# Score bursts in tiles of 64 rows by 64 columns, both row blocks of a part in turn

## The chip, the cores and the metric

One Trainium2 chip, one core. The metric is device time in microseconds. The profiler's span of an execution is about 1.9 us less than the time of the same execution (568.3 against 570.23 for the profiled run of before), so spans are compared with spans and times with times.

## The reference

Attention with a threshold, then a gated feed-forward layer, 8 batches x 8 heads x 576 rows, head size 64:

```python
scores = matmul(q, k.transpose(0, 1, 3, 2)) / sqrt(64)
scores = where(scores >= max(scores, -1) - tau, scores, -1e9)
attn   = exp(scores - max(scores, -1));  attn /= sum(attn, -1) + 1e-9
x      = matmul(attn, v)                  # to rows of 8 heads x 64 = 512
xn     = x / sqrt(mean(x * x) + 1e-6) * rms_g
out    = (silu(xn @ w_gate) * (xn @ w_val)) @ w_out     # 512 -> 1536 -> 512
```

Only `q @ k.T` is touched here. It is computed in fp32, since the threshold is sharp.

## The kernel before

The kernel lists its operations, orders them per engine in a scheduler of its own (`order_ops`) and then emits them in that order. One step is 128 rows of two heads: a "score burst" on TensorE fills two stretches of PSUM, `s_ps[0]` and `s_ps[1]`, one per head ("bank 0" and "bank 1" below); VectorE reads each (`ttr`: scale, minimum, copy to SBUF); GpSimd, ScalarE and VectorE make the weights from it. There are 144 steps: 128 of main rows, 16 of the last 64 rows of two batches.

```python
def emit_s(s):
    ...
    if kind == "m":      # 128 main rows: one row block
        outs = [(slice(0, 128), b % 2, lambda hs: qkT[b % 2][p][hs, 0, c])]
    else:                # last 64 rows of two batches: two row blocks, each with keys of its own
        outs = [... (HALF[e], e, lambda hs, e=e: qTv[b % 2][hs, p, HALF[e]]) ...]

    def fn(o):
        for rows, i, lhs in outs:
            for part in range(2):            # 576 keys in two parts of 288
                for h in range(2):           # the head: SBUF partitions 0-63 or 64-127
                    hs, n = HALF[h], S // 2
                    nc.tensor.matmul(s_ps[h][rows, ROW_AT + n * part:ROW_AT + n * part + n], lhs(hs),
                                     kT[i][p][h][hs, n * part:n * part + n], start=True, stop=True)

    for h in range(2):
        deps.append(ttr_of.get((s - 1, h)))   # VectorE must have read this bank of the step before
```

The contraction has 64 rows, so each head uses half the array's rows (a row tile) and the two heads run side by side. With 128 output rows the tile is 64 rows by 128 columns; with 64 it is 64 by 64, and two blocks of 64 output rows lie in two column tiles. (Where the texts speak of the "row tiles of a part in turn", they mean these row blocks.) Operations carry a `mode`: 1 for 64x128 tiles (main bursts and the fp32 transposes of q and k, L303, L438, L462 in the traces), 2 for bursts of the last rows, 0 and 3 for full-height products.

Of the kernel before, what the change touches and what calls it, by code (L numbers as in the profile page):

```python
# [24 lines left out]


class Op:
    __slots__ = ("eng", "cost", "prio", "deps", "fn", "ring", "frees", "slot", "end", "start", "dma", "opens", "nring", "mode", "bulk", "release", "pick")

    def __init__(self, eng, cost, prio, deps, fn, ring=None, frees=None, dma=0.0, nring=1, mode=0, bulk=False):  # L30
        self.eng, self.cost, self.prio, self.fn = eng, cost, prio, fn
        self.deps = [d for d in deps if d is not None]
        self.ring, self.frees, self.dma = ring, frees, dma
        self.slot = self.end = self.start = None
        self.opens = ()
        self.nring = nring
        self.mode = mode
        self.bulk = bulk
        self.release = 0.0
        self.pick = None  # L40


def order_ops(ops, ring_sizes):


    import heapq

    ring_free = {r: [(0.0, i) for i in range(n)] for r, n in ring_sizes.items()}
    users = {}
    left = {}  # L50
    for i, o in enumerate(ops):
        left[i] = len(o.deps)
        for d in o.deps:
            users.setdefault(id(d), []).append(i)
    pending = {}
    for i, o in enumerate(ops):
        pending.setdefault(o.eng, [])
        if not left[i]:
            pending[o.eng].append(i)
    eng_free = {e: 700.0 for e in pending}  # L60
    dma_free = 0.0
    mode = 0
    out = []
    ready_at = {i: 0.0 for i in range(len(ops))}
    while len(out) < len(ops):
        best = None
        for e, lst in pending.items():
            if not lst:
                continue
            t0 = eng_free[e]  # L70
            cand = None
            for i in lst:
                o = ops[i]
                t = max(t0, ready_at[i])
                if o.ring is not None:
                    free = [f for f in ring_free[o.ring] if o.pick is None or f[1] in o.pick]
                    if len(free) < o.nring:
                        continue
                    t = max(t, sorted(free)[o.nring - 1][0])
                other = e == "PE" and o.mode != mode  # L80
                t = max(t, o.release)
                if o.bulk:
                    t = max(t, dma_free - BACKLOG)
                k = (t + (BIAS if other else 0.0), o.prio, i)
                if cand is None or k < cand:
                    cand = k
            if cand is not None and (best is None or cand < best[0]):
                best = (cand, e)
        (t, _, i), e = best
        o = ops[i]  # L90
        cost = o.cost
        if e == "PE":
            if o.mode != mode:
                t -= BIAS
                cost += SWITCH
            mode = o.mode
        o.start = t
        if o.ring is not None:
            o.slot = []
            for _ in range(o.nring):  # L100
                got = min(f for f in ring_free[o.ring] if o.pick is None or f[1] in o.pick)
                ring_free[o.ring].remove(got)
                o.slot.append(got[1])
        eng_free[e] = t + cost
        if o.dma:
            dma_free = max(dma_free, t + 300.0) + o.dma
            o.end = max(dma_free, t + o.cost) + (LAT_TR if o.cost == COST["sp_tr"] else LAT_LD if o.bulk else 2000.0)
        else:
            o.end = t + cost
        if o.frees is not None:  # L110
            ring_free["R"].append((o.end + SEM, o.frees[0].slot[o.frees[1]]))
        for slot in o.opens:
            ring_free["R"].append((o.end + SEM, slot))
        pending[e].remove(i)
        out.append(o)
        for j in users.get(id(o), []):
            u = ops[j]
            wait = 0.0 if u.eng == o.eng and not o.dma else SEM + (SLACK if u.eng == "PE" else 0.0)
            ready_at[j] = max(ready_at[j], o.end + wait)
            left[j] -= 1  # L120
            if not left[j]:
                pending[u.eng].append(j)
    return out
# [3 lines left out]
def kernel(  # L127
# [26 lines left out]
    def sb(name, shape, dt=FP32):  # L154
        return konst.tile(shape, dt, tag=name, name=name)

    def ps(name, n):
        return psum.tile([128, n], FP32, tag=name, name=name)
# [14 lines left out]
    qkT = [[t[:, p].rearrange("p (j s) -> p j s", j=2)[:, :, 0:MAIN].rearrange("p j (c n) -> p j c n", n=128)  # L173
            for p in range(NP)] for t in qkt]
    kT = [[[t[:, p, S:2 * S], t[:, p, MAIN:MAIN + S]] for p in range(NP)] for t in qkt]
    kTt = [[t[:, :, S + MAIN:2 * S], t[:, :, MAIN:S]] for t in qkt]
    qTv = [sb(f"qTv{i}", [128, NP, 128]) for i in range(2)]
# [30 lines left out]
    ring = [ps(f"ring{i}", 512) for i in range(4)]  # L208
    ring += [s_ps[h][:, 512 * i:512 * (i + 1)] for h in range(2) for i in range(2)]
    HALF = (slice(0, 64), slice(64, 128))  # L210
# [9 lines left out]
    def add(eng, cost, prio, deps, fn, **kw):  # L220
        o = Op(eng, cost, prio, deps, fn, **kw)
        ops.append(o)
        return o
# [11 lines left out]
    for s, (ci, p) in enumerate(steps):  # L235
        kind, b, _ = chunks[ci]
# [309 lines left out]
    def emit_s(s):  # L546
        ci, p = steps[s]
        kind, b, c = chunks[ci]
        if kind == "m":
            deps = qk_ready[b, p, c] + kt_ready[b, p]  # L550

            outs = [(slice(0, 128), b % 2, lambda hs: qkT[b % 2][p][hs, 0, c])]
        else:
            deps = list(qv_ready[b])
            outs = []
            for e in range(2):
                deps += qk_ready[2 * b + e, p, 0] + kt_ready[2 * b + e, p]
                outs.append((HALF[e], e, lambda hs, e=e: qTv[b % 2][hs, p, HALF[e]]))

        def fn(o):  # L560
            for rows, i, lhs in outs:
                for part in range(2):
                    for h in range(2):

                        hs, n = HALF[h], S // 2
                        nc.tensor.matmul(s_ps[h][rows, ROW_AT + n * part:ROW_AT + n * part + n], lhs(hs),  # L566
                                         kT[i][p][h][hs, n * part:n * part + n], start=True, stop=True)

        for h in range(2):
            deps.append(ttr_of.get((s - 1, h)))  # L570
        o = add("PE", COST["s_main" if kind == "m" else "s_virt"], s, deps, fn, mode=1 if kind == "m" else 2)
        if REL_N[0] <= s < REL_N[1]:
            o.release = REL[0] + REL[1] * s
        if kind == "m":
            last_s[("k", b, p)] = [o]
        else:
            last_sv[b, p] = [o]
            for e in range(2):
                last_s.setdefault(("k", 2 * b + e, p), [])
                last_s["k", 2 * b + e, p] = last_s["k", 2 * b + e, p] + [o]  # L580
        return o
# [327 lines left out]
    for c in range(DFF // 512):  # L909
        for d in range(0, 4, 2):  # L910
            for w_dram, w_sb in ((moe_w_gate, wg), (moe_w_val, wv)):
                slot = n // 2 % len(stage)
# [20 lines left out]
    for j in range(4):  # L933
        o = add("POOL", COST["pool_dma"], W_FROM + W_STEP * n + j + WO_AT, [], lambda o, j=j: nc.gpsimd.dma_start(
            out=wo[:, 3 * j:3 * j + 3], in_=wo_src[:, 3 * j:3 * j + 3]), dma=DMA_NS['wo'], bulk=True)
# [3 lines left out]
    for s, (ci, p) in enumerate(steps):  # L939
        kind, b, c = chunks[ci]  # L940
        so = s_of[s] = emit_s(s)
        emit_softmax(s, so)
        if p % 2:
            emit_av(s)
        if p == NP - 1:
            gi, j = place[ci]
            xt_op[ci] = emit_x(ci, s, gi % NXT, 128 * j)
            if ci in last_of:
                g = groups[last_of[ci]]
                emit_ffn(last_of[ci] % NXT, [(ci_of[x], xt_op[ci_of[x]]) for x in g], s + (ELAG if place[ci][0] < NELAG else LAG), PACE,  # L950
                         last_of[ci] >= len(groups) - STREAMED)
            for bb in ([b] if kind == "m" else [2 * b, 2 * b + 1]):
                left[bb] -= 1
                if not left[bb] and bb + 2 < B:
                    emit_batch_inputs(bb + 2)
# [4 lines left out]
    for h in range(2):  # L960
        ttr_of[len(steps) - 1, h].opens = OPENS[h]
    seq = order_ops(ops, {"R": 4})
    global LAST_SEQ
    LAST_SEQ = seq
    with tc.manual_schedule():
# [77 lines left out]
```

## Time and profile before

| | before |
|---|---|
| time, median of 3 runs | 567.91 us (567.86 to 568.21) |
| span of the profiled execution | 568.3 us |
| TensorE busy, share of the chain that ended last | 98%, 89% |
| score bursts (L566) in that chain | 28% |
| VectorE waiting for score bursts | 60.5 us |

The chain is the work that ended last, followed back from the last instruction to whatever released each step. A record is one pass of a matmul in the trace, and a start stamp is its recorded start. A row of groups reads: line, engine, operation, out<-in, tile (rows*columns), shape, count, then busy us and mean ns, then idle time before it and what ended it. The prediction shows the rows themselves.

### The profile page before, as it was taken

What the parts mean: (1) busy time and instruction counts of PE and PEld (TensorE: products, weight loads), DVE (VectorE), ACT (ScalarE), POOL (GpSimd) and SP (SyncE); (2) the same over time, 40 slices, a digit from 0 to 9 for tenths busy, and PEclk for the clock granted to TensorE, in tenths of its full rate; (3) what the DMA queues carried; (4) which work ended last, traced back from release to release, by engine and by line L of the source; (5) the groups of instructions that cost most, each with busy time, mean ns of one, the idle gap of its engine ahead of it and who ended that gap; (6) DMA issues with size and microseconds to landing.
All of it is one profiled execution on the core that took longest, in us unless ns stands there. A gap on an engine that the chain in (4) does not pass through costs nothing.

```text
span 568.3 us, 13686 instructions
## 1 busy us (share of the span) xinstructions
PE 558.4 (98%) x5000; PEld 334.7 (59%) x5000; DVE 427.2 (75%) x1093; ACT 457.4 (80%) x739; POOL 322.4 (57%) x462
## 2 busy tenths in 40 slices
PE   8999999999999999999999999999999999999997
PEld 4666766767676555555555555545555455454674
DVE  4899977969958588758895789659875886586354
ACT  4999899999878787979898898778978897884332
POOL 2378946976747457666766658555666555551000
PEclk9999999999999999999999999999999999999999
DMA  8999998769994686999876799789887565633211
GB/s 187 250 289 282 178 195 184 161 132 202 167 202 104 136 159 149 177 177 187 178 160 148 142 186 181 161 168 162 174 167 184 88 96 86 178 81 44 84 37 38
DMA packets 270019, 88.98 MB, mean 157 GB/s; under 512 B 252544, under 2 KB 262272, under 8 KB 269952
## 3 DMA queue, kind: packets, MB, share of 16 engines
q1 hardware_dynamic: 267168, 86.02, 74.1%
q0 software_dynamic: 1600, 1.57, 1.8%
q8 instruction: 39, 0.64, 0.5%
q10 hardware_dynamic: 1184, 0.52, 0.3%
q14 instruction: 28, 0.23, 0.1%
HBM read 37.75 MB, written 9.44 MB: 83 GB/s over the span
## 4 chain that ended last, share of the span: by engine, by line
PE 89%; DVE 3%; DMA 2%; issue 2%; ACT 2%; POOL 1%; SPq 0%; DVEq 0%; POOLq 0%; ACTq 0%
PE s_ps L566 28%; PE ring L792 16%; PE ring L797 16%; PE ring L853 14%; PE ring L697 6%; PE ring L303 2%; PE ring L693 2%; DVE ssb L589 2%; DMA qkn<-in_q_dram 1%; PE s_ps L831 1%; PE s_ps L853 1%; PE ring L659 1%; PE s_ps L797 1%; PE ring L364 1%; DMA stage<-in_q_dram 1%
## 5 line engine op out<-in xcount | busy, mean ns | idle before, releaser
L589 DVE CUSTOM_DVE_ANT_0 ssb<-s_ps,zrow 128x576 f32<-128x576 f32 x288 | 207.8, 754 | 67.7 <-PE s_ps L566 60.5
L607 ACT ACTIVATE ssb<-ssb,nth 128x576 f32<-128x576 f32 x224 | 165.9, 766 | 32.4 <-POOL nth L596 32.1
L566 PE MATMUL s_ps<-qkt 64*128 64x288 f32 x1024 | 170.2, 429 | 1.4 <-DVE mx L589 1.1
L566 PEld LDWEIGHTS s_ps<-qkt 64*128 64x128 f32 x1024 | 96.2, 186 | 53.5 <-DVE mx L589 16.2
L640 POOL TENSOR_SCALAR wsb<-ssb,nth 128x576 f16<-128x576 f32 x64 | 110.5, 1726 | 9.7 <-DMA wt<-wsb 2.9
L792 PE MATMUL ring<-xnT,wg 128*128 128x512 f16 (+1 forms) x548 | 112.9, 328 | 0.4 <-DVE sl L809 0.4
L797 PE MATMUL ring<-xnT,wv 128*128 128x256 f16 (+1 forms) x544 | 111.4, 327 | 0.6 <-ACT qTv L472 0.3
L596 POOL TENSOR_SCALAR nth<-mx 128x2 f32<-128x2 f32 x144 | 31.6, 220 | 133.9 <-DVE mx L589 120.6
L809 DVE SCALAR_TENSOR_TENSOR sl<-th,ring 128x512 f32<-128x512 f32 (+1 forms) x137 | 75.9, 554 | 25.9 <-ACT th L806 24.6
L614 ACT ACTIVATE wsb<-ssb 128x1152 f16<-128x1152 f32 x80 | 92.9, 1161 | 1.9
L806 ACT ACTIVATE th<-ring 128x512 f32<-128x512 f32 (+1 forms) x137 | 66.3, 486 | 28.9 <-PE ring L792 26.4
L853 PE MATMUL ring<-wo,hf 128*128 128x512 f16 x384 | 89.3, 380 | 0.0
L645 POOL TENSOR_TENSOR wsb<-wsb,esb 128x576 f16<-128x576 f16 x64 | 81.8, 1278 | 8.8 <-ACT esb L626 4.4
L814 DVE TENSOR_TENSOR hf<-ring,sl 128x256 f16<-128x256 f32 (+1 forms) x136 | 75.9, 558 | 10.0 <-PE s_ps L566 0.5
L797 PEld LDWEIGHTS <-wv 128*128 128x128 f16 x576 | 52.2, 98 | 42.9 <-issue 12.3
L792 PEld LDWEIGHTS <-wg 128*128 128x128 f16 x576 | 52.0, 98 | 41.0 <-issue 11.6
L853 PEld LDWEIGHTS <-hf 128*128 128x128 f16 x408 | 37.4, 98 | 47.2 <-issue 6.6
L626 ACT ACTIVATE esb<-ssb,nth 128x576 f16<-128x576 f32 x64 | 49.2, 768 | 7.1 <-POOL nth L596 7.0
L697 PE MATMUL ring<-va,wt 128*128 128x65 f16 (+1 forms) x1264 | 52.8, 193 | 0.0
L697 PEld LDWEIGHTS <-wt 128*128 128x128 f16 (+1 forms) x1280 | 48.7, 100 | 3.4
L611 ACT ACTIVATE wsb<-ssb 128x576 f16<-128x576 f32 x64 | 43.6, 681 | 1.6
L693 PE MATMUL ring<-va,wt 128*128 128x130 f16 (+1 forms) x158 | 35.1, 227 | 0.1
(68 smaller groups left out, 448.1 us busy)
## 6 DMA issues: line engine op xcount, KB each, us to landing
vst<-in_v_dram SPq DMA_DIRECT2D x32, 256.0 KB, 3.2
qkn<-in_k_dram SPq DMA_DIRECT2D x31, 256.0 KB, 3.8
out_dram<-osb SPq DMA_DIRECT2D x31, 256.0 KB, 2.6
qkn<-in_q_dram SPq DMA_DIRECT2D x28, 256.0 KB, 4.1
stage<-in_moe_w_gate_dram SPq DMA_DIRECT2D x6, 512.0 KB, 6.6
stage<-in_moe_w_val_dram SPq DMA_DIRECT2D x6, 512.0 KB, 6.3
wt<-wsb SPq DMA_TRANSPOSE x128, 3.1
wo<-in_moe_w_out_dram POOLq DMA_DIRECT2D x4, 384.0 KB, 7.6
```

The lines of the kernel that those rows point to most:

```text
L566: nc.tensor.matmul(s_ps[h][rows, ROW_AT + n * part:ROW_AT + n * part + n], lhs(hs), kT[i][p][h][hs, n * part:n * part + n], start=True, st ...
L589: nc.vector.tensor_tensor_reduce(out=ssb[a][:, h], in0=s_ps[h][:, ROW_AT:ROW_AT + S], in1=zrow, scale=-1.0 / 8.0, scalar=3.0e38, op0=ALU.a ...
L607: nc.scalar.activation(out=ssb[a][:, h], in_=ssb[a][:, h], func=PRELU, scale=-1.0, bias=nth[m][:, h:h + 1], **PRELU_KW)
L614: nc.scalar.activation(out=wsb[s % NW], in_=ssb[a], func=AF.Exp)
L640: nc.gpsimd.tensor_scalar(out=wsb[s % NW][:, h], in0=ssb[a][:, h], scalar1=nth[m][:, h:h + 1], scalar2=None, op0=ALU.is_le)
L645: nc.gpsimd.tensor_tensor(out=wsb[s % NW][:, h], in0=wsb[s % NW][:, h], in1=esb[es], op=ALU.mult)
L697: nc.tensor.matmul(ring[o.slot[0]][rs, at:at + D + 1], w[:, 5 * h + j, rs], va[vi][:, p, 2 * j + h], start=False, stop=(h == 1 and j == 3))
L792: nc.tensor.matmul(ring[o.slot[0]][:, 0:n], wg[d][:, fs], xnT[slot][:, d, 0:n], start=(d == 0), stop=(d == 3))
L797: nc.tensor.matmul(ring[o.slot[0]][:, 0:n], wv[d][:, fs], xnT[slot][:, d, 0:n], start=(d == 0), stop=(d == 3))
L809: nc.vector.scalar_tensor_tensor(out=sl[i][:, 0:n], in0=th[i][:, 0:n], scalar=1.0, in1=ring[g.slot[0]][:, 0:n], op0=ALU.add, op1=ALU.mult)
L814: nc.vector.tensor_tensor(out=hf[hi][:, 0:n], in0=ring[vv.slot[0]][:, 0:n], in1=sl[i][:, 0:n], op=ALU.mult)
L853: nc.tensor.matmul(ring[(first or o).slot[0]], hf[hs[fc][0]][:, 128 * j:128 * (j + 1)], wo[:, fc], start=(fc == 0), stop=(fc == NFC - 1))
```

## The change

The intent: a burst with no 64x128 transposes behind it leaves the tiling in any case, so it may as well use the tiles of the last rows' bursts, whose first weight load is half as wide. Both row blocks of a part now come in turn.

```diff
         if kind == "m":
-            outs = [(slice(0, 128), b % 2, lambda hs: qkT[b % 2][p][hs, 0, c])]
+            whole = [(slice(0, 128), b % 2, lambda hs: qkT[b % 2][p][hs, 0, c])]
+            quads = [(rs, b % 2, lambda hs, rs=rs: qkT[b % 2][p][hs, 0, c, rs]) for rs in HALF]
 ...
         def fn(o):
-            for rows, i, lhs in outs:
-                for part in range(2):
+            for part in range(2):
+                for rows, i, lhs in quads if kind == "v" or o.quad else whole:
                     for h in range(2):
 ...
     seq = order_ops(ops, {"R": 4})
+    on_pe = [o for o in seq if o.eng == "PE"]
+    for o, after in zip(on_pe, on_pe[1:]):
+        o.quad = after.mode != 1
```

More of the change, by code (lines that the diff above doesn't have):

```diff
@@ L27 @@
 class Op:
-    __slots__ = ("eng", "cost", "prio", "deps", "fn", "ring", "frees", "slot", "end", "start", "dma", "opens", "nring", "mode", "bulk", "release", "pick")
+    __slots__ = ("eng", "cost", "prio", "deps", "fn", "ring", "frees", "slot", "end", "start", "dma", "opens", "nring", "mode", "bulk", "release", "pick", "quad")
     def __init__(self, eng, cost, prio, deps, fn, ring=None, frees=None, dma=0.0, nring=1, mode=0, bulk=False):
@@ L40, in __init__ @@
         self.pick = None
+        self.quad = False
 def order_ops(ops, ring_sizes):
@@ L550, in emit_s @@
             deps = qk_ready[b, p, c] + kt_ready[b, p]
-            outs = [(slice(0, 128), b % 2, lambda hs: qkT[b % 2][p][hs, 0, c])]
+            whole = [(slice(0, 128), b % 2, lambda hs: qkT[b % 2][p][hs, 0, c])]
+            quads = [(rs, b % 2, lambda hs, rs=rs: qkT[b % 2][p][hs, 0, c, rs]) for rs in HALF]
         else:
             deps = list(qv_ready[b])
-            outs = []
+            quads = []
             for e in range(2):
                 deps += qk_ready[2 * b + e, p, 0] + kt_ready[2 * b + e, p]
-                outs.append((HALF[e], e, lambda hs, e=e: qTv[b % 2][hs, p, HALF[e]]))
+                quads.append((HALF[e], e, lambda hs, e=e: qTv[b % 2][hs, p, HALF[e]]))
         def fn(o):
-            for rows, i, lhs in outs:
-                for part in range(2):
+            for part in range(2):
+                for rows, i, lhs in quads if kind == "v" or o.quad else whole:
                     for h in range(2):
```

## The prediction

> **What bounds the kernel now.** I read the page first, its head, its busy shares and its chain that ended last, because a change to one engine's instructions is worth something only where that engine sets the end.
>
> ```profile
> span 568.3 us, 13686 instructions
> PE 558.4 (98%) x5000; PEld 334.7 (59%) x5000; DVE 427.2 (75%) x1093; ACT 457.4 (80%) x739; POOL 322.4 (57%) x462
> PE 89%; DVE 3%; DMA 2%; issue 2%; ACT 2%; POOL 1%; SPq 0%; DVEq 0%; POOLq 0%; ACTq 0%
> ```
>
> TensorE (PE) is busy 98% of the span and carries 89% of the chain; the next engine, ScalarE, is busy 80%. The granted clock is full in all 40 slices. The ends of matmuls are modelled, so 98% alone would prove little, and I work with starts only. Next, the table of groups with shapes kept apart, to see what the score bursts (L566) cost and what waits there.
>
> ```profile
> L566 PE MATMUL s_ps<-qkt 64*128 64x288 f32 x1024 | 170.2, 429 | 1.4 <-DVE mx L589 1.1
> L566 PE MATMUL s_ps<-qkt,qTv 64*64 64x288 f32 x256 | 19.4, 415 | 0.0
> L566 PEld LDWEIGHTS s_ps<-qkt 64*128 64x128 f32 x1024 | 96.2, 186 | 53.5 <-DVE mx L589 16.2 <-issue 12.7 <-DVE xsb L715 4.2
> L566 PEld LDWEIGHTS s_ps<-qkt,qTv 64*64 64x64 f32 x256 | 8.9, 132 | 6.9 <-DVE mx L589 1.7 <-issue 1.5 <-DVE xsb L715 1.1
> ```
>
> The 64*128 and 64*64 name the tile, rows by columns: 128 bursts run as 64 by 128, 8 records each (four fp32 matmuls, two weight loads and two passes per matmul), and the 16 bursts of the last rows run as 64 by 64, 16 records each. So the form that the change wants for most bursts is in the old trace already. That is the best thing that a blind prediction can find: a measurement of the new code on the same chip. I therefore compare the two forms between the same neighbours, in the chain in order of time around 305 to 310 us.
>
> ```profile
> 304.74 1.17 PE s_ps L566 x8
> 305.91 2.70 PE ring L853 x12
> 308.61 1.14 PE s_ps L566 x16
> 309.75 0.32 PE ring L853
> ```
>
> Both stand before the same product with 128 by 128 tiles. 8 records in 64x128 take 1.17 us of the chain; 16 records in 64x64 take 1.14 us. Twice the instructions take 0.03 us less, so the four tiles must run at once. The timeline, cut to narrow windows, shows how. Columns: first start, time to the last modelled end, and how many records had begun when the window closed. The first three are one whole burst, cut at 304.72, 305.06 and 305.30; the others one 64x64 burst, cut at 308.539, 308.555, 308.565, 308.60 and 308.89.
>
> ```profile
> 304.67 0.51 PE L566 MATMUL s_ps<-qkt 64*128 64x288 f32 x2
> 304.67 0.76 PE L566 MATMUL s_ps<-qkt 64*128 64x288 f32 x4
> 304.67 1.00 PE L566 MATMUL s_ps<-qkt 64*128 64x288 f32 x6
> ...
> 308.54 0.45 PE L566 MATMUL s_ps<-qkt,qTv 64*64 64x288 f32 x1
> 308.54 0.46 PE L566 MATMUL s_ps<-qkt,qTv 64*64 64x288 f32 x2
> 308.54 0.48 PE L566 MATMUL s_ps<-qkt,qTv 64*64 64x288 f32 x3
> 308.54 0.49 PE L566 MATMUL s_ps<-qkt,qTv 64*64 64x288 f32 x4
> 308.54 0.73 PE L566 MATMUL s_ps<-qkt,qTv 64*64 64x288 f32 x8
> ```
>
> The whole burst goes in pairs, one per row tile; the other goes in fours. From the start stamps in the trace: whole burst, first to second round 346 ns, then 243 and 242 ns, and 7 ns from the first to the second row tile, so first start to last start 838 or 839 ns in every burst that had no wait inside. 64x64: first to second round 293 ns, then 243 and 242 ns, the four tiles starting at 0, 7, 27 and 34 ns, so 811 or 812 ns in all 16. From the last start to the next 128x128 matmul it is 335 ns after either form, and from the last matmul of the product before to the burst's first 309 ns (512 columns) for either.
>
> **What the Trainium skill says.** "TensorE: Matmul & The Clock Gate", section "LDWEIGHTS (loading the stationary operand)": a load takes its columns divided by 1.2 GHz, whatever its rows. For 128 against 64 columns that is 107 against 53 ns, a difference of 53; the trace's first round is 346 - 293 = 53 ns shorter. It agrees. Later loads hide under the 242 ns of the pass before, in both forms.
> The same page, "What overlaps and what doesn't", has loads overlapping only where the row group differs, and matmuls in strict program order. This trace does not agree for column tiles: the old code writes all four matmuls of the first 64 rows before those of the other 64. In strict order those are eight records in four rounds, then four rounds more, some 53 + 7 x 242 = 1747 ns; the trace has 812.
> "TensorEngine Tiling (Array Packing)", "Key Properties": changing the tiling mode drains the engine. The trace agrees: from the last start of a whole burst to the first transpose (L303, the same 64x128 tiles) it is 236 ns, from a 64x64 burst to that transpose 333 ns. A change of mode costs some 97 ns.
> "Perfetto Trace Analysis", "Tensor Engine Instruction (MATMUL, LD_WEIGHTS)": starts are recorded, ends estimated.[...]
>
> **The change part by part.** The scheduler's sequence is untouched: row for row, the built programs hold the same instructions and waits on VectorE, ScalarE, GpSimd and the DMA queue. On TensorE, of the 144 bursts 97 turn into 64x64 form, 31 stay whole because an operation in 64x128 tiles follows, and the 16 of the last rows keep their tiles but change order. Each of the 97 has four matmuls more (388 in all); both waits stay on its first two matmuls.
>
> (a) Smaller first load: 839 - 812 = 27 ns less per burst. It is made of 53 ns less of loading, less the 27 ns by which the second column tile starts later.
> (b) New order. The 27 ns are the time in which TensorE takes four matmuls, 6.7 ns each. With both row tiles of a part in turn, the second column tile's first matmul is third in the order, not fifth, so it should start 13 ns after the first, and the last tile at 20, not 34. That is 13.5 ns more per burst, my estimate from those stamps. First to last start would be 53 + 242 x 3 + 20 = 799 ns, against 839: 40 ns less.
> (c) 97 x 40 ns = 3.9 us, and 16 x 13.5 ns = 0.2 us in the last rows' bursts.
> (d) Three of the 97 have transposes in 64x128 tiles just before (the rule looks only at what follows): each gets a change of mode that it hadn't, 3 x 97 ns = 0.3 us lost.
> Sum: 3.9 + 0.2 - 0.3 = 3.8 us, if each nanosecond lay on the path.
>
> How much of it does? From 60 to 510 us TensorE is busy 448.5 of 450 us (sums by stretch), but waits hide inside bursts: in 31 of 144 bursts the second row tile's first matmul waits for VectorE's read of the bank from the step before, 12.2 us together, most of it (8.7 us) in the first 80 us. A release of this kind moves forward only with what feeds VectorE; the part of the saving made just before can be eaten by it. After the release the burst still has its load and four rounds to do, so it saves its own 40 ns. VectorE itself waits 60.5 us for L566 and is not full, so it follows when the burst ends sooner. I take 10% off: 3.4 us. 567.9 - 3.4 = 564.5 us, 0.6%.
>
> **The rivals.**
> First, twice the instructions cost time: if the four tiles ran two at a time, 16 records were eight rounds, 4 x 242 = 0.97 us more per burst and 94 us in all, some 660 us. Against it: all 16 old bursts of that form. For it: there the two column tiles read different keys, here both stream the same ones; a clash on those reads can't be excluded, but I see no sign of it. I give it 1 to 2%.
> Second, the order does nothing: if the tiles start in an order of the engine's own making, part (b) is nil, and the sum is 97 x 27 = 2.6 less 0.3, times 0.9: 2.1 us, 565.8 us. The even spacing of 0, 7, 27, 34 speaks for the order of the program; I give this rival a quarter.
> Third, the saved time turns into waits: VectorE's 754 ns per bank and two banks per step need at least 1.5 us of each step, and a burst cannot begin in a bank not yet read. Then the waits inside bursts grow by what was saved, and the time stays near 567.5. Against it: from 60 to 510 us L566 has 880 + 256 records, which is 110 + 16 steps, 3.6 us each, far above 1.17 + 1.5 us, so this chain has slack except where the order bunches steps. It can take a part, not all.
> Fourth, a gain beyond the sum, by waits that vanish. The 3.5 us of waits after 80 us set its limit, and I expect none of it.
>
> **Range and chances.** Full sum without loss: 564.1. Rival two: 565.8. Rival three in part: 566. So 564.5, with 563.6 to 566.2 for 8 in 10. Two per cent would be 11.4 us, three times what the parts can give; faster by that 1%, slower 1.5% for the clash of reads.
>
> **What would show it.** Right: 1800 or so records of L566 in 64x64 form; first to last start near 799 ns in undisturbed 64x64 bursts; pieces of 1.13 us or a little under where the chain now has 1.17; 335 ns to the next product unchanged; the three bursts behind transposes starting about 97 ns later than now; busy time of VectorE and ScalarE the same. If (b) is wrong, first to last start is 812. Wrong altogether: rounds of two in the new bursts, or waits inside bursts well above 12 us. The sum would also be wrong if the whole bursts that stay became longer.

## The result, and the profile after

The changed kernel took 565.6 us (median of 6 runs, 565.38 to 565.91), before 567.88 us (6 runs, 566.68 to 568.94) in the same rounds. The ratio is 0.9962, with a 95% interval of 0.9949 to 0.9975; a ratio is always the mean time of one kernel's fast runs over that of the other's of the same rounds, so not quite the ratio of the medians. That is a change of less than 2%, and inside the predicted range of 563.6 to 566.2; the saving is 2.2 us by the ratio, where 3.4 was named.

The lines of the new page that answer to those of before; L569 is now the score burst:

```profile
span 563.5 us, 15238 instructions
PE 555.4 (99%) x5776; PEld 316.9 (56%) x5776; DVE 426.6 (76%) x1093; ACT 456.8 (81%) x739; POOL 322.6 (57%) x462
PE 93%; DVE 3%; DMA 1%; ACT 1%; issue 1%; POOL 1%; DVEq 0%; POOLq 0%
```

The spans (568.3 and 563.5) differ by more than the times do. The control below has 566.4: the profiled execution of before was one of its slower ones, and two spans alone would have flattered the change. The groups with shapes kept apart:

```profile
L569 PE MATMUL s_ps<-qkt 64*64 64x288 f32 x1552 | 127.4, 416 | 1.5 <-DVE mx L592 1.4
L569 PE MATMUL s_ps<-qkt 64*128 64x288 f32 x248 | 41.0, 429 | 0.3 <-DVE mx L592 0.3
L569 PE MATMUL s_ps<-qkt,qTv 64*64 64x288 f32 x256 | 19.2, 415 | 0.0
```

1552 records are 97 bursts of 16, 248 are 31 of 8, 256 are the 16 of the last rows: the counts of the prediction. (L569 has 97 x 8 = 776 records more, and 5776 - 5000 is 776.) Now the chain in order of time, at the same place in the program as before's piece, a burst of main rows first:

```profile
301.49 1.13 PE s_ps L569 x16
302.62 2.70 PE ring L856 x12
305.32 1.13 PE s_ps L569 x16
```

Both kinds take 1.13 us, where they took 1.17 and 1.14. The timeline of the first of them, cut at 301.424, 301.431, 301.438 and 301.46 us, shows the four tiles beginning within 20 ns, not 34:

```profile
301.42 0.45 PE L569 MATMUL s_ps<-qkt 64*64 64x288 f32 x1
301.42 0.46 PE L569 MATMUL s_ps<-qkt 64*64 64x288 f32 x2
301.42 0.47 PE L569 MATMUL s_ps<-qkt 64*64 64x288 f32 x3
301.42 0.47 PE L569 MATMUL s_ps<-qkt 64*64 64x288 f32 x4
```

From the start stamps in the trace, an undisturbed burst now has its tiles at 0, 7, 14 and 20 ns, rounds of 293, 243 and 243 ns, and 797 to 800 ns from first to last start, in main and last rows alike. From the last start to the next full-height product it is 335 ns, as before.

Where did the time go? I split both traces at the starts of the same bursts (counted from 0). In the last column is what the prediction's terms give for the bursts in that stretch: 40 ns for each converted one, 13.5 for each of the last rows.

| stretch, burst to burst | before (two executions) | changed (three executions) | the terms give |
|---|---|---|---|
| 0 to 13 | 38.20, 38.16 | 38.28, 41.41, 39.24 | -0.44 |
| 13 to 24 | 34.50, 34.62 | 34.56, 34.56, 34.60 | -0.40 |
| 24 to 40 | 54.45, 54.46 | 53.97, 53.96, 54.22 | -0.49 |
| 40 to 56 | 61.25, 59.69 | 59.98, 60.66, 60.24 | -0.29 |
| 56 to 88 | 112.98, 113.16 | 111.65, 111.65, 111.65 | -0.84 |
| 88 to 143 | 198.59, 198.58 | 197.02, 197.03, 197.02 | -1.59 |

(The second execution of before and the second and third of the changed kernel are the control and repeats below. The terms here are (a) and (b); the cost of transposes ahead, (d), falls on bursts 10, 13 and 99.) From burst 88 on, where little waits (0.34 us inside three bursts before, 0.26 us in two after), the gain is 1.57 us against 1.59: the terms are right to a few nanoseconds per burst (burst 99, with transposes ahead, gained 19 ns of its 40, as a wait inside it shrank). From 56 to 88 it is 1.3 to 1.5 us, more than the sum, since two waits shrank: the one inside burst 66, from 395 to 83 ns, and one ahead of it, by 185 and 356 ns against the two executions of before. In the first 24 bursts there is no gain at all: the waits inside bursts, 8.7 and 9.0 us there in the two executions of before, are 9.8 to 10.6 us in the three after. In 0 to 13 the changed kernel even shows two longer executions. The experiments had two questions: is each term of the sum what I said it is, and what eats the saving of the first 24 steps?

### The profile page after: what moved, and what is told of

It reads as the page before. It is cut to its first block, busy times and chain, and to the rows that moved or that the text cites. A ratio compares the mean times of both kernels' runs of the same rounds, so it can differ in the third digit from the quotient of the medians.

```text
span 563.5 us, 15238 instructions
## 1 busy us (share of the span) xinstructions
PE 555.4 (99%) x5776; PEld 316.9 (56%) x5776; DVE 426.6 (76%) x1093; ACT 456.8 (81%) x739; POOL 322.6 (57%) x462
## 3 DMA queue, kind: packets, MB, share of 16 engines
q0 software_dynamic: 1600, 1.57, 1.8%
## 4 chain that ended last, share of the span: by engine, by line
PE 93%; DVE 3%; DMA 1%; ACT 1%; issue 1%; POOL 1%; DVEq 0%; POOLq 0%
PE s_ps L569 29%; PE ring L795 17%; PE ring L800 16%; PE ring L856 15%; PE ring L700 6%; PE ring L304 2%; PE ring L696 2%; DVE ssb L592 2%; DMA stage<-in_moe_w_gate_dram 1%; PE s_ps L834 1%; PE s_ps L856 1%; PE s_ps L800 1%; PE ring L365 1%; PE ring L662 1%; PE s_ps L262 1%; PE s_ps L795 1%
## 5 line engine op out<-in xcount | busy, mean ns | idle before, releaser
L569 PE MATMUL s_ps<-qkt 64*64 64x288 f32 (+1 forms) x1800 | 168.3, 417 | 1.8 <-DVE mx L592 1.7
L643 POOL TENSOR_SCALAR wsb<-ssb,nth 128x576 f16<-128x576 f32 x64 | 110.5, 1727 | 12.3 <-DMA wt<-wsb 5.4
L569 PEld LDWEIGHTS s_ps<-qkt 64*64 64x64 f32 (+1 forms) x1800 | 79.1, 140 | 63.9 <-DVE mx L592 19.1
```

Source lines behind the costliest of these rows:

```text
L643: nc.gpsimd.tensor_scalar(out=wsb[s % NW][:, h], in0=ssb[a][:, h], scalar1=nth[m][:, h:h + 1], scalar2=None, op0=ALU.is_le)
```

## The experiments

Three jobs of four kernels with five rounds each, one chip per job; the kernels of a job share the runs of before. Bursts are called small (64x64) or whole (64x128).

| run | median, us | before, same rounds | ratio, 95% interval |
|---|---|---|---|
| e6_before | 569.06 | 568.87 | 1.0006, 0.9983 to 1.0029 |
| e1_after | 567.55 | 568.87 | 0.9976, 0.9954 to 0.9998 |
| e4_late | 566.96 | 568.87 | 0.9961, 0.9940 to 0.9982 |
| e5_early | 569.96 | 568.87 | 1.0018, 0.9991 to 1.0046 |
| e2_old_order | 568.32 | 568.73 | 0.9995, 0.9976 to 1.0015 |
| e3_all | 571.26 | 568.73 | 1.0049, 1.0027 to 1.0071 |
| e7_both | 567.50 | 568.73 | 0.9981, 0.9961 to 1.0000 |
| e8_cols32 | 570.35 | 568.73 | 1.0019, 0.9989 to 1.0049 |
| f1_bank_then_col | 566.75 | 569.74 | 0.9947, 0.9926 to 0.9968 |
| f2_bank_first | 567.31 | 569.74 | 0.9948, 0.9923 to 0.9972 |
| f3_before_bank_first | 568.60 | 569.74 | 0.9986, 0.9965 to 1.0006 |
| f4_after | 566.54 | 569.74 | 0.9946, 0.9927 to 0.9965 |

All outputs are right. On these chips equal programs spread more than on the first one (before: 567.17 to 570.92 in the first job), so differences under about 1 us are decided here by start stamps, not by times.

### The control and the repeat: e6_before, e1_after

Edits: none. The kernel before against itself, and the changed kernel once more.

> The kernel before against itself, a control. Ratio 1.000 in every theory; what it shows is how far the ratio of two equal programs strays in five rounds, and in its trace how much of the distance between the first two profiles (568.3 against 563.5 us) was the one execution of before that happened to be profiled. I expect a ratio within 0.998 to 1.002 and a profile nearer 566 us than 568.

> The changed kernel again, to narrow the gain. Theory A (each of the late bursts saves its 40 ns in full, those of the first 80 us save nothing because they wait for VectorE and for loads): 76 x 40 ns + 16 x 13.5 ns - 0.1 us = 3.2 us, ratio 0.9944. Theory B (the waits eat a third of the saving everywhere): 2.3 us, ratio 0.996. Theory C (all of it arrives, the first 80 us too): 3.8 us, ratio 0.9933.

The control came out at 1.0006, and its interval of 0.23% either way is the resolution of one job. The repeat gained 0.24%, 1.4 us. The first measurement had 2.2, the repeat of the third job (f4_after) 3.1; the mean of the three ratios is 0.9961, 2.2 us. The times fit theory B, but the stretches above do not have its shape: after burst 24 the saving is whole, and before it there is none.

The long first stretch of e1_after (41.41 us from burst 0 to 13) has a visible cause. Its timeline:

```profile
36.28 0.46 PE L304 MATMUL ring<-id,qkn 64*128 64x64 f32 x8
37.92 0.46 PE L304 MATMUL ring<-id,qkn 64*128 64x64 f32 x8 [1.18 <-DMA qkn<-in_q_dram]
```

TensorE stood 1.18 us for a load of q; the products just after took 0.65 us in place of 0.41 for the same eight records, and the mean granted clock of that execution was 0.997. A late load, then a granted clock of 0.57 from 38 to 42 us. That the wait lowered the clock is not shown: in the first execution of before, TensorE waited 0.76 us for the load of q at that place, and the clock stayed at 1.00.

### Where the saving counts: e4_late, e5_early

```diff
+    step_of = {id(o): s for s, o in s_of.items()}
 ...
-        o.quad = after.mode != 1
+        o.quad = after.mode != 1 and step_of.get(id(o), 0) >= 24    # e4_late;  e5_early: < 24
```

> Only bursts from step 24 on (80 us and later) take the 64x64 form, 76 of the 97; the last rows keep the new order. Theory A: the same time as the whole change, 3.2 us less than before. Theory B: 76/97 of the whole change's gain. Theory C: 0.8 us slower than the whole change. A fourth theory D, that the small form in the first 80 us does harm (more instructions where the queue waits at VectorE): faster than the whole change by up to 0.8 us.

> Only the 21 bursts before step 24 take the 64x64 form; the last rows have the new order. Theory A: 0.2 us less than before, all of it from the last rows, so a ratio of 0.9996 and not to be told from 1. Theory C: 0.2 + 0.8 - 0.2 = 0.8 us less, 0.9986. Theory D: slower than before by up to 0.8 us, 1.0005 to 1.001.

The small form in the late bursts alone gained 0.39%, which is also the mean of the whole change's three measurements; in the early ones alone it gained nothing, and the two intervals do not touch. So the 0.8 us that the sum credits to the first 24 steps is not there (against theory C). Theory D, that it harms there, was suggested by the times (1.0018 for e5_early, but with 1 inside its interval) and called for a look at the traces.

### What the early small bursts change: a wait inside the burst

From burst 13 to burst 18, e4_late and both executions of before took 14.26 or 14.27 us; e5_early, e3_all and all three executions of the changed kernel took 15.11. So exact a difference is no noise. In burst 14, bank 1 comes free 0.68 us after bank 0, because VectorE reads one after the other. The lines below are from VectorE's timeline, its read of bank 0 of that burst: start, duration, and in the bracket its idle time and what ended it. First e4_late, where burst 14 is whole:

```profile
48.61 0.76 DVE L592 CUSTOM_DVE_ANT_0 ssb<-s_ps,zrow 128x576 f32<-128x576 f32 x1 [0.26 <-PE s_ps L569]
```

The changed kernel:

```profile
49.74 0.76 DVE L592 CUSTOM_DVE_ANT_0 ssb<-s_ps,zrow 128x576 f32<-128x576 f32 x1 [0.69 <-PE s_ps L569]
```

And f1_bank_then_col, which is told below:

```profile
48.51 0.76 DVE L592 CUSTOM_DVE_ANT_0 ssb<-s_ps,zrow 128x576 f32<-128x576 f32 x1 [0.24 <-PE s_ps L569]
```

The bursts began at 46.99, 47.69 and 46.91 us, so VectorE began 1.62, 2.05 and 1.60 us after. The start stamps say why. A whole burst does both passes of its first matmul (bank 0, all 128 rows) before the second matmul's wait; bank 0's last record starts at 1029 ns. In the changed kernel the second matmul in the order is again bank 1's, but the first covers only 64 rows: the other 64 rows of bank 0 stand third, behind a wait that is not theirs. Bank 0's last record starts at 1463 ns. Two rounds of 242 ns less the smaller load's gain come to the 0.43 us by which VectorE is later.

### The order of banks and columns: f1_bank_then_col, f2_bank_first, f3_before_bank_first, f4_after

```diff
 f1:         for part in range(2):
-                for rows, i, lhs in quads if ... else whole:
-                    for h in range(2):
+                for h in range(2):
+                    for rows, i, lhs in quads if ... else whole:
 f2: as f1, and in steps under 24 all of bank 0 before bank 1; small only if the operation ahead isn't mode 1 either
 f3: the kernel before, in main steps under 24:  for h in range(2):  for part in range(2):
 f4: the changed kernel
```

> The changed kernel with one more swap in the order: within a part first both column tiles of bank 0, then both of bank 1. Theory W (in a burst that waits inside for bank 1, program order holds the second column tile of bank 0 behind that wait, so VectorE gets bank 0 some 0.43 us later than from a whole burst): bank 0's last matmul starts about 992 ns after the burst's first in a burst whose bank 1 comes 680 ns late (changed kernel 1458, kernel before 1029); the stretch from burst 13 to burst 18 falls from 15.11 to about 14.4 us; undisturbed bursts stay at 798 ns; the time is 0.5 to 1.2 us below the changed kernel's. Rival L (the first 80 us lose because more instructions have to be fetched or taken while loads saturate the DMA): nothing moves, 15.11 us and the changed kernel's time.

> The version that the experiments point to: 64x64 form where neither neighbour is in 64x128 tiles; in the first 24 steps all of bank 0 before all of bank 1, later part by part, in each part bank 0's column tiles first. Theory W: bank 0's last matmul starts near 785 ns in the first 24 steps whatever bank 1 waits for, burst 13 to 18 takes 14.0 to 14.3 us, and the time is 3 to 4 us below before, 0.8 to 1.5 below the changed kernel. Rival L: no better than the changed kernel. Rival S (ScalarE sets the pace of the first 16 steps, whatever TensorE does): not below 14.27 us, so no better than the other order.

> The kernel before with nothing but this in the first 24 steps: both parts of bank 0 before those of bank 1, whole bursts. A dose of theory W without any 64x64 tile: bank 0's last matmul starts at 832 ns in place of 1029 where bank 1 comes late. W without a limit: burst 13 to 18 falls from 14.27 to 13.7 to 14.1 us. Rival S: 14.27 us as before. In both the whole time moves by less than 0.6 us, under the noise, so the trace decides.

> The changed kernel again, beside the two reorderings on the same chip: ratio 0.996 to 0.998 to before, burst 13 to 18 15.11 us as in its other two profiles.

| kernel | bank 0's last start in burst 14, ns | burst 13 to 16, us | 13 to 18 | 13 to 24 |
|---|---|---|---|---|
| f2_bank_first | 785 | 7.82 | 14.48 | 33.99 |
| f3_before_bank_first | 832 | 7.90 | 14.18 | 34.68 |
| f1_bank_then_col | 990 | 8.05 | 14.77 | 34.33 |
| before (both executions), e4_late | 1029 to 1031 | 8.10 to 8.11 | 14.26 to 14.27 | 34.50 to 34.62 |
| the changed kernel, f4_after | 1463 | 8.92, 8.92 | 15.11 | 34.56, 34.60 |

Theory W passes where it speaks: the later bank 0 is finished, the longer the three steps from 13 to 16, in order through all five rows, and the kernel before obeys it too (f3), with no small tile in it. The runs left out of the table mostly agree: e3_all and e5_early lie on the last row, e2_old_order and e8_cols32 just beyond it (1474 and 1468 ns, 9.01 and 9.03 us). But e7_both, whose burst 13 is whole as in f2, takes 8.71 us at 1464 ns, so burst 14 is not all of it. Rival L, that instructions or their fetching are the cause, is out: f1 has as many matmuls as the changed kernel. But my numbers for 13 to 18 were too hopeful: f1 took 14.77, not 14.4, f2 14.48, not 14.0 to 14.3, f3 14.18, not 13.7 to 14.1; two steps later part of the gain is spent again. So rival S, that ScalarE sets the pace at 14.27 whatever TensorE does, is not out as a floor: only f3 came below it, by 0.09. Over 13 to 24 even the 0.8 us of the changed kernel are gone: 34.56 against 34.50 and 34.62.

What ends that stretch is not TensorE. GpSimd's timeline around 56 to 71 us, only the first and last line of the stretch, for the kernel before:

```profile
56.03 0.19 POOL L729 TENSOR_SCALAR irm<-ssq 128x1 f32<-128x1 f32 x1
...
70.41 0.52 POOL L596 TENSOR_SCALAR nth<-mx 128x2 f32<-128x2 f32 x2
```

And for the changed kernel:

```profile
55.87 0.19 POOL L732 TENSOR_SCALAR irm<-ssq 128x1 f32<-128x1 f32 x1
...
70.26 0.52 POOL L599 TENSOR_SCALAR nth<-mx 128x2 f32<-128x2 f32 x2
```

Between these lines GpSimd works back to back in both (masks of 1.74 us, products of 1.28 us, casts, two DMA issues of 0.86 and 0.83 us): 14.38 and 14.39 us, 14.38 in the control and 14.40 in e4_late. The last line makes the thresholds of steps that ScalarE waits for (1.92 us in before, 1.15 in the changed kernel, where TensorE's part had come later), VectorE waits for ScalarE, and burst 22 for VectorE. In all 14 profiled executions burst 22 begins 16.9 to 17.0 us after the first of these lines. The stretch is not 34.6 us in every run with small early bursts, and the difference is again GpSimd's: e5_early took 36.88 and e3_all 35.68, where GpSimd waited 2.7 and 1.2 us for loads of weights before that line; whether the small bursts delay those loads is not shown. Before that, from 8 to 48 us, ScalarE is busy 35.6 of 40 us in before (VectorE 34.6): in the first 16 steps it masks both banks as well as taking their exponentials. That these engines pace the first 24 steps is read from the traces; no run took work from them to prove it.

In time, f1, f2 and f4 cannot be told apart: 0.9947, 0.9948, 0.9946, where f1 and f2 were expected 0.5 to 1.5 us below f4. The version that the experiments pointed to (f2) is thus no faster than the change as far as this can be measured, and its one profiled execution was a slow one (span 568.7).

### The order of tiles alone: e2_old_order

```diff
-            for part in range(2):
-                for rows, i, lhs in quads if kind == "v" or o.quad else whole:
+            for rows, i, lhs in quads if kind == "v" or o.quad else whole:
+                for part in range(2):
```

> The whole change, but in each burst all four matmuls of rows 0 to 63 before those of rows 64 to 127, as the last rows had it. My theory (the engine takes a matmul every 6.7 ns in program order, and a tile starts when its first has been taken): first to last start of an undisturbed burst 811 to 812 ns in place of 798, starts of the four tiles at 0, 7, 27, 34 ns, and some 113 x 13.5 ns = 1.5 us more than the changed kernel. Rival (the engine orders tiles by itself): 798 ns and the changed kernel's time.

First to last start is 811 to 812 ns in undisturbed bursts, and the tiles of the burst at 303.62 us start at 0, 6, 26 and 33 ns. From burst 88 to 143 it takes 197.65 us, 0.63 more than the changed kernel; that stretch has 37 small main bursts and 8 of last rows, and 45 x 13.5 ns is 0.61. So term (b) is confirmed by itself, and the engine takes matmuls in program order at 6.7 ns each. In time the job saw 0.9995 against before; the 1.5 us to the changed kernel fits (e7_both of the same job: 0.9981), but not sharply.

### All bursts small: e3_all

```diff
-        o.quad = after.mode != 1
+        o.quad = True
```

> All 128 bursts take the 64x64 form, also the 31 that an operation in 64x128 tiles follows. My theory (a change of mode costs 97 ns between any two tilings): each of the 31 saves 40 ns and pays 97, so 31 x 57 ns = 1.8 us slower than the changed kernel, the last start of such a burst to the transpose behind it 333 ns in place of 236. Rival (the drain is paid only for going to or from 128 rows): 31 x 40 ns = 1.2 us faster than the changed kernel.

The chain through one burst with transposes behind it, in this run:

```profile
293.94 1.13 PE s_ps L569 x16
295.07 0.64 PE ring L304 x16
```

The same burst in the changed kernel, where it is whole:

```profile
290.15 1.17 PE s_ps L569 x8
291.33 0.49 PE ring L304 x16
```

That is 1.77 against 1.66 us. By the stamps, the first transpose comes 333 or 334 ns after the last start behind every burst of this kind, in place of 235 to 243 where nothing overlaps. A change from 64x64 to 64x128 costs 98 ns there, and the rival is out. The expectation missed a second part: the transposes come in pairs, and the second pair now starts 110 to 113 ns after the first behind most of these bursts, in place of 55 to 57, and 52 or so later behind the others too; sixteen of them take 487 to 490 ns from first to last start, not 435 to 440. Why is not shown. Less the 40 ns that the burst saves, each costs some 110 ns, not 57. From 88 to 143 it took 198.18 us, 1.16 more than the changed kernel, and the 10 bursts of this kind in that stretch make 1.09 of it (what else differs nearly cancels). For all 31 it would be 3.4 us; the time, 0.49% over before where 0.998 or so is the changed kernel, is about 4 us worse, twice what I expected. The rule in the change is right, by more than its arithmetic.

### Both neighbours: e7_both

```diff
-    for o, after in zip(on_pe, on_pe[1:]):
-        o.quad = after.mode != 1
+    for ahead, o, after in zip(on_pe, on_pe[1:], on_pe[2:]):
+        o.quad = after.mode != 1 and ahead.mode != 1
```

> The 64x64 form only where neither the operation behind nor the one ahead is in 64x128 tiles: some 94 bursts in place of 97. My theory: each of the three saves 97 and gives back 40 ns, 0.17 us in all if on the path, but two of them are in the first 50 us, where waits decide; so 0 to 0.17 us faster than the changed kernel, under the noise. It is the best version that my reading points to.

110 small bursts in place of 113. The three behind transposes begin 58 or 59 ns after the last transpose; in the changed kernel it is 151 or 152. So term (d) is 93 ns each. In time nothing is to be seen (0.9981), as expected.

### Narrower still: e8_cols32

```diff
+    QUARTER = tuple(slice(32 * x, 32 * x + 32) for x in range(4))
 ...
-    quads = [(rs, ..., qkT[b % 2][p][hs, 0, c, rs]) for rs in HALF]       # 64 columns
+    quads = [(rs, ..., qkT[b % 2][p][hs, 0, c, rs]) for rs in QUARTER]    # 32 columns
```

> The converted bursts in tiles of 64 rows by 32 columns, 16 matmuls a burst, eight tiles at once, four row tiles of a part in turn. My theory (first load = [...]27 ns, then 3 rounds of 242 after the first of 240, and the last of eight tiles starts 7 x 6.7 = 47 ns after the first): 27 + 726 + 47 = 800 ns from first to last start, against 798: the changed kernel's time within 0.3 us. Rival 1 (the smaller load alone counts): 772 ns, 2.5 us faster. Rival 2 (eight tiles can't all run, or taking 32 loads and 32 passes in time fails): rounds longer than 242 ns, up to twice, 30 to 90 us slower.

The burst that answers to the one at 301.42 us in the changed kernel, 32 records now:

```profile
308.20 1.20 PE L570 MATMUL s_ps<-qkt 64*32 64x288 f32 x32
```

First to last start is 799 ns in the median and 798 in the least, the first round 267 ns (26 less than with 64 columns; half of the 53 ns between 128 and 64 columns would be 27), the eight tiles starting at 0, 7, 14, 20, 27, 34, 40 and 47 ns. All eight run at once; what the load saves, the later start of the last tiles spends, as computed. From burst 88 to 143 it took 197.08 us, 0.06 from the changed kernel. The time was worse (570.35, spread 567.68 to 572.51), because of the first 13 bursts (41.38 us in the profiled execution, with 0.9 us of waiting for a load of q and 1.6 us for ScalarE) and of waits from 40 to 88; whether the small tiles cause that is open.

## Why the prediction was right, and where it was off

The predicted time held within its range, and its mechanism step by step:

- Part (a), smaller first load: right. First round 293 in place of 346 ns; with the old order 811 to 812 ns from first to last start (e2_old_order).
- Part (b), new order: right to a nanosecond or two. 797 to 800 ns, 799 predicted; 0.63 us for 45 bursts, 0.61 computed.
- Part (c), the sum over bursts: right wherever TensorE sets the pace: 1.57 us against 1.59 from burst 88 on.
- Part (d), transposes ahead: 93 ns, predicted 97. But the sum also credits these three bursts with 40 ns each, and that is wrong: directly behind transposes a whole burst without a wait took 786 ns from first to last start (burst 10 of before and of e4_late), less than the small form's 798. The prediction's "838 or 839 ns in every burst that had no wait inside" overlooked it.
- The rivals: two tiles at a time, with both streaming the same keys, is refuted by the 243 ns rounds; an order of the engine's own making by e2_old_order.
- Its third rival came true in part: the waits inside bursts grew from 12.2 us (12.3 in the control) to 14.0 (13.5 and 13.8 in the other two executions), nearly all of it in the first 24 bursts.
- Luck, inside the range: the waits in and ahead of burst 66 became shorter, so that 56 to 88 gained 0.5 to 0.7 us more than the sum. This is the fourth rival, of which nothing was expected.

The mis-sized step is "I take 10% off: 3.4 us". Measured over three jobs it was 2.2 us of the 3.8, so some 40% off. The prediction reasoned that a burst saves its own 40 ns after a release. That is true of the burst, but in the first 24 steps it is not the burst that ends the stretch: 13 to 24 takes 34.6 us with or without the change, paced by GpSimd and ScalarE as the traces read, which the shares over the whole span (57% and 80%) hide. That takes 21 of 97 bursts out of the sum. The prediction also missed that the order of the small matmuls puts half of bank 0 behind bank 1's wait; it cost VectorE 0.43 us in burst 14, though most of that lay in slack (from 13 to 24, f1 and f2 took 0.2 and 0.6 us less than the changed kernel). Without the 21 bursts 3.2 us are left, and the traces from burst 24 on show at least that, burst 66 included: 426.6 us in the mean of two executions before (427.28 and 425.89), 423.0 in that of three after (422.61, 423.31 and 423.13). Single executions stray, though: e4_late, the same from burst 24 on, took 424.76.

What stays open is the remaining microsecond, between those 3.2 us or more and the 2.2 in the mean of the times. It may lie in the first 13 bursts, where executions differ by over 3 us with late loads, or between bursts 40 and 56, where all 14 executions range from 59.69 to 62.28 us (61.78 in e4_late, where ScalarE waited 2.5 us for GpSimd's thresholds and VectorE for ScalarE). In the first 13, the four executions with whole bursts (f3_before_bank_first among them) took 37.91 to 38.78 us, the ten with small ones 38.13 to 41.41. The difference may be the small form or chance; the late-only kernel, with the narrowest spread of its job (566.10 to 567.35), speaks for the first, but no run settles it.

## What to carry to other kernels

Look in the old trace for the new form of an operation: sixteen bursts of it, compared from start to start between equal neighbours, gave the gain to a few nanoseconds, and only the share that counts was left to guess. For that share, split the span into stages and ask in each which engine works back to back; a busy share over the whole hides a stage in which another one leads. And when a wide instruction is split, put all the pieces of what is free ahead of the first piece that waits, or the queue's order will hold them behind a wait that isn't theirs; here that was worth 0.2 us or more in one stretch, and nothing that the times could show.

## What the Trainium skill lacked or had wrong

- "TensorE: Matmul & The Clock Gate", "What overlaps and what doesn't": loads overlapping only across row groups, and matmuls in strict order, don't hold across column tiles. With all of one column tile's matmuls first, the other's still begin 27 ns after (e2_old_order and the kernel before), and 16 records take 812 ns, not the 1747 of strict order. Order does bind at a wait: what stands behind a waiting matmul stood still, also for another column tile (0.68 us in burst 14).
- The same page, "Measured speedup vs the span model", gives about 4 ns per further tile. For fp32, with two loads and two passes to a matmul, the runs show 6.7 ns: four tiles over 20 ns, eight over 47.
- "TensorEngine Tiling (Array Packing)", "Key Properties", says that a change of mode drains the engine and gives no figure: 93 to 98 ns between 64x128 and 64x64, in both directions (58 to 151 ns ahead of a burst, 236 to 334 behind it), and some 52 ns more among the transposes behind a burst (e3_all).
